# Sketched attention feeding a squared-ReLU layer: loads and stores by t, w_out in 8 KB rows, and nd in four banks

## The chip, the cores and the metric

The kernel runs on one core of a Trainium2 chip. The metric is the device time of one execution in microseconds (us), the median of several runs. Engines are named as the profile names them: PE is the matrix engine (PEld its weight loads), DVE the vector engine, ACT the scalar engine, POOL is GpSimd, and SP the engine that issues most DMAs. Line numbers (L526) are those of the kernel before.

## What is computed

Every head's q and k pass through a degree-two sketch with r = 8: phi(x) is the outer product of S1·x and S2·x, 64 features. Attention is linear in phi(k), its denominator is a dot product, and the four heads of 32 side by side are the input of a two-matrix layer with relu squared.

```python
# batch 4, heads 4, seq 1088, head_dim 32; d_model 128, d_ff 2048
def phi(x):
    a = einsum('rd,bhsd->bhsr', S1, x); b = einsum('rd,bhsd->bhsr', S2, x)
    return einsum('bhsi,bhsj->bhsij', a, b).reshape(..., 64)
kv  = einsum('bhsf,bhsd->bhfd', phi(k), v);  z = phi(k).sum(axis=2)
num = einsum('bhsf,bhfd->bhsd', phi(q), kv); den = einsum('bhsf,bhf->bhs', phi(q), z) + 1e-06
x = (num / den).transpose(0, 2, 1, 3).reshape(4352, 128)
h = x @ w_in                       # 4352 x 2048
out = relu(h)**2 @ w_out           # 4352 x 128, float32
```

## The kernel before

**Tiles.** A sequence of 1088 is written as 32 blocks t of 34 rows j; a partition is (head, t). j is 32 regular rows and two left over. The tokens are cut into nine chunks: two of 512 columns for each batch, and chunk 8 of 256 with the left-over rows of all batches.

**The order.** All work after the setup is one list, `ORDER`, written out by hand. Each item names a helper, its indices and, after `@`, the engine of a copy, relu or square (A for ACT, V for DVE; `M` on a square S means one DVE instruction over two pairs). The engines run their own instructions strictly in the order of the list, and semaphores hold them where data or a buffer is missing. An item that waits therefore holds everything behind it on its engine.

**Keys of batch b.** kT transposes k on DVE (L236), ka multiplies by the sketch matrix Wk (L259), kc copies out of PSUM, kp forms the outer products on DVE (L289), kv multiplies them by v on PE (L339), and kt, kr, kx bring the result into KV. kg, gs, wz, wc make the denominator's weights: a Gram matrix (L306), then a product with `S2bd`, the block-diagonal S2 (L313), written into Wq.

**Queries of batch b** (b = 4 stands for the left-over rows). qT transposes q, qa multiplies (L411), qc copies, dt, dr and da form the denominator and divide, qf forms the outer products (L477) and qp transposes them back (L490).

**Join.** `nd(ci, p)` multiplies KV by the query features in 32 x 32 pieces of the array (L526), two row groups by four column groups, into two PSUM banks. Chunks 0, 1 and 8 take two calls (p = 0, 1), chunks 2 to 7 one each. xe copies the result to `xT` in bf16 (L543 to L548).

**Layer.** `M(ci, u)` makes two of the 16 blocks of 128 hidden columns (L556), R takes the relu (L576 on ACT, L578 on DVE), S squares (L587, L589), `O(ci, u)` accumulates the output (L599), E copies it out (L611) and stores it (L616, L622). PSUM's eight banks are two h buffers of two banks (`ps_h`), one output bank and three others (`ps_m`). W is an idle matmul.

**Loads.** SP issues for each batch k, q and the v of heads 0 and 1, one DMA per head with the four row groups i outermost (L133). GpSimd's queue brings the v of heads 2 and 3 and v's left-over rows (L139): for batch 0 ahead of the two weight matrices (L158, L160), for batches 1 to 3 behind them, issued from within kp (L297). `w_out` is laid out with row ct·128 + c on partition c, 16 pieces of 512 B of the source in each; both weights are cast to bf16 on the way. S1, S2 and the four diagonal blocks of `S2bd` come through ACT's queue (L118, L119, L172); a DVE copy (L197) repeats S for the heads.

```python
526  nc.tensor.matmul(nds[l][32 * h : 32 * h + 32, d0 : d0 + n],
         KV[rows, be, f, 32 * h : 32 * h + 32], src[rows, 2 * h + f, c0 : c0 + n],
         start=(f == 0), stop=(f == 1))
556  nc.tensor.matmul(t[:, i, :N], w_in_sb[:, 2 * u + i, :], T["x", ci][:, :N], ...)
```

## Time and profile before

| | |
|---|---|
| median of the runs | 116.22 us (116.17 to 117.56) |
| the profiled execution, its own time | 116.08 us |
| its span, first to last instruction | 114.3 us |
| first hidden-layer matmul (M.0.0, L556) | 19.67 us into the span |
| last output copy, E.8 (L611), and its stores' issue | ends at 109.66 us, issued at 109.69 us |
| PE / DVE / ACT / GpSimd busy | 101.0 / 94.3 / 87.4 / 12.8 us |
| moved by DMA | 10.23 MB, mean 89 GB/s |
| w_in / w_out, issue to landing | 8.1 / 22.3 us |
| relu on ACT, 128 x 1024 | 61 of 1039 ns |
| output matmuls (L599) | 544 of 219 ns in the row |

The page of a profile gives the busy time of each engine, then the span in 40 slices (2.86 us each) with the busy share in tenths. Matmuls are pipelined, so a row's mean duration is longer than the distance from one to the next. Where an engine stood idle, a wait names what ended it: "A <- B: 2.2, 1, 2.2" is 2.2 us in total, once, the longest 2.2 us. The chain is followed backward from the last instruction to whatever released each step. A line of the stage table gives a stretch of the span, its length, the busy time of PE, PEld, DVE, ACT and POOL with counts, the granted PE clock, the mean share of the 16 DMA engines that were busy, and GB/s.

### The profile page before, as it was taken

What the parts mean: (1) busy time and instruction counts of PE and PEld (TensorE: products, weight loads), DVE (VectorE), ACT (ScalarE), POOL (GpSimd) and SP (SyncE); (2) the same over time, 40 slices, a digit from 0 to 9 for tenths busy, and PEclk for the clock granted to TensorE, in tenths of its full rate; (3) what the DMA queues carried; (4) which work ended last, traced back from release to release, by engine and by line L of the source; (5) the groups of instructions that cost most, each with busy time, mean ns of one, the idle gap of its engine ahead of it and who ended that gap; (6) DMA issues with size and microseconds to landing.
All of it is one profiled execution on the core that took longest, in us unless ns stands there. A gap on an engine that the chain in (4) does not pass through costs nothing.

```text
span 114.3 us, 4082 instructions
## 1 busy us (share of the span) xinstructions
PE 101.0 (88%) x1806; PEld 72.2 (63%) x1806; DVE 94.3 (83%) x148; ACT 87.4 (76%) x140; POOL 12.8 (11%) x24
## 2 busy tenths in 40 slices
PE   5297679987999989999999999999999997999920
PEld 1173556653778864787977557857757866779810
DVE  6185999989929999999999999999899988099700
ACT  4132315999599998799889999899999698895920
POOL 6968200002800000000000000000000000000000
PEclk9999999999999999999999999999999999999995
DMA  4999999977542002000200012002101112012032
GB/s 95 305 202 281 279 280 225 217 209 257 144 139 88 28 9 62 27 0 14 68 21 0 0 17 80 6 6 54 37 0 19 73 16 72 14 11 77 14 58 75
DMA packets 7152, 10.23 MB, mean 89 GB/s; under 512 B 3424, under 2 KB 4704, under 8 KB 7136
## 3 DMA queue, kind: packets, MB, share of 16 engines
q1 hardware_dynamic: 3344, 7.67, 22.8%
q0 software_dynamic: 3616, 2.24, 11.9%
q8 instruction: 14, 0.23, 0.8%
q10 hardware_dynamic: 176, 0.07, 0.2%
q14 instruction: 2, 0.02, 0.0%
HBM read 8.79 MB, written 2.23 MB: 96 GB/s over the span
## 4 chain that ended last, share of the span: by engine, by line
PE 59%; DMA 19%; ACT 10%; POOL 5%; issue 3%; POOLq 0%; ACTq 0%
PE o_ps L599 23%; PE h_ps L556 22%; DMA v_in<-in_v_dram 19%; PE nd_ps L526 7%; ACT r_sb L576 6%; PE acc_ps L339 3%; PE qab_ps L411 3%; ACT g_sb L587 2%; POOL v_in L133 2%; PE gg_ps L306 1%; POOL w_out_sb L160 1%; POOL v_in L139 1%; ACT osb L611 1%; PE kr_ps L363 1%; ACT kab L277 1%
## 5 line engine op out<-in xcount | busy, mean ns | idle before, releaser
L576 ACT ACTIVATE r_sb<-h_ps 128x1024 bf16<-128x1024 f32 (+1 forms) x67 | 63.2, 999 | 5.8 <-PE h_ps L556 5.3
L556 PE MATMUL h_ps<-xT,w_in_sb 128*128 128x512 bf16 (+1 forms) x144 | 39.0, 368 | 0.6 <-ACT r_sb L576 0.6
L599 PEld LDWEIGHTS <-g_sb 128*128 128x128 bf16 x544 | 33.7, 98 | 9.0 <-DVE g_sb L589 0.4
L599 PE MATMUL o_ps<-w_out_sb,g_sb 128*128 128x128 bf16 x544 | 37.3, 219 | 0.0
L589 DVE TENSOR_TENSOR g_sb<-r_sb 128x1024 bf16<-128x1024 bf16 (+2 forms) x41 | 36.4, 922 | 0.5 <-ACT r_sb L576 0.3
L556 PEld LDWEIGHTS <-w_in_sb 128*128 128x128 bf16 x144 | 11.7, 99 | 6.9 <-issue 3.0
L289 DVE TENSOR_TENSOR kp<-kab 128x1024 f32<-128x1024 f32 (+1 forms) x8 | 10.6, 1337 | 0.0
L490 DVE STREAM_TRANSPOSE qp<-qf 128x1024 f32<-128x1024 f32 (+1 forms) x9 | 10.4, 1174 | 0.1
L526 PE MATMUL nd_ps<-qp,KV 32*32 32x256 f32 (+2 forms) x416 | 10.1, 299 | 0.4 <-ACT r_sb L576 0.3
L477 DVE TENSOR_TENSOR qf<-aq,qab 128x1024 f32<-128x1024 f32 (+1 forms) x9 | 10.2, 1154 | 0.1
L587 ACT ACTIVATE g_sb<-r_sb 128x1024 bf16<-128x1024 bf16 (+1 forms) x9 | 8.9, 1016 | 0.1
L526 PEld LDWEIGHTS nd_ps<-qp,KV 32*32 32x32 f32 x416 | 5.5, 104 | 4.5 <-issue 1.7
L339 PE MATMUL acc_ps<-kp,v_in 128*32 128x64 f32 x288 | 5.7, 221 | 2.5 <-DMA v_in<-in_v_dram 2.4
L339 PEld LDWEIGHTS acc_ps<-kp,v_in 128*32 128x32 f32 x288 | 4.6, 110 | 4.3 <-DMA v_in<-in_v_dram 3.0
L411 PE MATMUL qab_ps<-Wq,qT 128*64 128x96 f32 x128 | 6.2, 249 | 0.7 <-issue 0.5
L236 DVE STREAM_TRANSPOSE kT<-k_in 128x1024 f32<-128x1024 f32 (+1 forms) x5 | 5.0, 1019 | 2.2 <-DMA k_in<-in_k_dram 2.2
L259 PEld LDWEIGHTS kab_ps<-Wk,kT 128*64 128x64 f32 x136 | 5.4, 159 | 1.9 <-DVE kT L236 1.3
L139 POOL DMA_DIRECT2D v_in<-in_v_dram x8 | 4.6, 581 | 16.8 <-DMA w_out_sb<-in_moe_w_out_dram 14.1
L411 PEld LDWEIGHTS qab_ps<-Wq,qT 128*64 128x64 f32 x128 | 5.5, 137 | 1.6 <-issue 0.6
L194 PE MATMUL idle_ps<-idle 128*128 128x512 bf16 x13 | 5.3, 508 | 1.2 <-DVE mask L166 1.2
L428 ACT COPY qab<-qab_ps 128x384 f32<-128x384 f32 (+1 forms) x9 | 4.1, 460 | 2.8 <-PE qab_ps L411 2.8
L578 DVE TENSOR_SCALAR r_sb<-h_ps 128x1024 bf16<-128x1024 f32 (+1 forms) x5 | 5.1, 1010 | 1.1 <-PE h_ps L556 1.1
(57 smaller groups left out, 70.4 us busy)
## 6 DMA issues: line engine op xcount, KB each, us to landing
k_in<-in_k_dram SPq DMA_DIRECT2D x4, 544.0 KB
q_in<-in_q_dram SPq DMA_DIRECT2D x4, 544.0 KB
out_dram<-osb SPq DMA_DIRECT2D x8, 256.0 KB
v_in<-in_v_dram POOLq DMA_DIRECT2D x8, 128.0 KB, 13.8
v_in<-in_v_dram SPq DMA_DIRECT2D x8, 128.0 KB
w_in_sb<-in_moe_w_in_dram POOLq DMA_DIRECT2D x1, 512.0 KB, 8.1
w_out_sb<-in_moe_w_out_dram POOLq DMA_DIRECT2D x1, 512.0 KB, 22.3
v_in<-in_v_dram POOLq DMA_DIRECT2D x8, 16.0 KB, 6.3
```

The costliest lines, as they stand in the source:

```text
L139: dma.dma_start(out=vraw[b][32 * j2 : 32 * (j2 + 1), :, NLO, :], in_=v[b].rearrange("h (t j) d -> j t h d", j=NJ)[32 + j2],)
L289: tt.tensor_tensor(out=t[:, :n], in0=s[:, 0, :n, :, None].to_broadcast([128, n, r, r]), in1=s[:, 1, :n, None, :].to_broadcast([128, n, r, r]),
L339: nc.tensor.matmul(acc[32 * h : 32 * h + 32, :64], vraw[b][:, h, 4 * gi + m, :], t[:, m * H + h].rearrange("p i j -> p (i j)"), start=(gi ...
L411: nc.tensor.matmul(t[64 * c : 64 * c + 64, m * H * W3 : (m + 1) * H * W3], cols, Wq[:, be].rearrange("p h x -> p (h x)"), start=True, stop ...
L477: nc.vector.tensor_tensor(out=t[:, :n], in0=T["aq", b][:, g0 : g0 + n, :, None].to_broadcast([128, n, r, r]), in1=T["qab", b][:, g0 : g0 + ...
L490: nc.vector.transpose(T["qp", b][:, :, 128 * i : 128 * i + 32 * nm].rearrange("p f (m t) -> p m f t", t=32), T["qf", b, i][:, : nm * H].re ...
L526: nc.tensor.matmul(nds[l][32 * h : 32 * h + 32, d0 : d0 + n], KV[rows, be, f, 32 * h : 32 * h + 32], src[rows, 2 * h + f, c0 : c0 + n], st ...
L556: nc.tensor.matmul(t[:, i, :N], w_in_sb[:, 2 * u + i, :], T["x", ci][:, :N], start=True, stop=True,)
L576: pin(nc.scalar.activation(t, h, ACTF.Relu))
L587: pin(nc.scalar.activation(t, s, ACTF.Square))
L589: pin(nc.vector.tensor_mul(t, s, s))
L599: nc.tensor.matmul(T["o", ci][:, m, :], T["g", ci, u // 2][:, 2 * (u % 2) + i, m * 128 : (m + 1) * 128], w_out_sb[:, ct, :], start=(ct == ...
```

## The change

- **v** is loaded by SP alone, each batch after its k and q: four DMAs, one for each 32 partitions (i), with t outermost and the heads within, and two for the left-over rows.
- **Outputs** of chunks 0 to 7 go out in four DMAs of 32 partitions with t outermost instead of one with i outermost; chunk 8's two halves are cut by t instead of by batch.
- **w_out** has row c·16 + ct on partition c, one run of 8 KB of the source in each. So that hidden unit c·16 + ct is block ct, M takes w_in's columns with a step of 16. A one-element GpSimd copy makes the weights wait for batch 0's k.
- **nd** computes four row groups at once into four banks: two of `ps_m` and one h buffer. For chunks 2 to 7 one call serves two chunks, for 0, 1 and 8 one call replaces two. xe picks its two banks.
- **S1, S2** are repeated for the heads by the DMA itself. `S2bd` comes from a matmul of a selection matrix with S and a masked copy (bd); the four DMAs into it, and the memsets of it and `Gs`, go. kg's second product takes 32 rows instead of 128.
- **ORDER** is written anew; kT.0.0, wk, bd and wq are now items of it, chunk 3's hidden work starts before chunk 2's, and some relus, squares and copies change engine.

The code, with ORDER cut to its beginning, up to the first hidden matmuls, and the one pair of chunks that swaps places:

```diff
-kT.0.0 kT.0.1 W.2 ka.0.0 kc.0.0 qT.0 ka.0.1 kc.0.1 W.2 kg.0 gs.0 kp.0.0 W.1 wz.0 wc.0 qa.0.0
-qa.0.1 kp.0.1 qc.0.0@A dt.0.0 dr.0.0 da.0.0 kv.0.0 qc.0.1@A qf.0.0 kv.0.1 kt.0 W.1 kr.0 kx.0@A
-qp.0.0 kT.1.0 W.3 nd.0.0 nd.0.1 xe.0.0@A xe.0.1@A ka.1.0 kc.1.0 M.0.0 R.0.0@A ka.1.1 dt.0.1
-kc.1.1 M.0.1 M.0.2 R.0.1@A kg.1 dr.0.1 da.0.1 qf.0.1 qp.0.1 gs.1 nd.1.0 wz.1 qT.1 R.0.2@A M.0.3
...
+kT.0.0 wk.0 W.3 ka.0.0 kT.0.1 bd.0 qT.0 wq.0 kc.0.0 ka.0.1 kc.0.1 W.2 kg.0 gs.0 W.1 wz.0 kp.0.1
+wc.0 kp.0.0 qa.0.0 qc.0.0@A kv.0.0 kv.0.1 qa.0.1 kt.0 dt.0.0 dr.0.0 kT.1.0 da.0.0 ka.1.0 qf.0.0
+qp.0.0 ka.1.1 qc.0.1@A dt.0.1 kr.0 kc.1.1 kc.1.0 kg.1 kx.0@A gs.1 nd.0 xe.0@A qT.1 wz.1 W.2
+M.0.0 M.0.1 R.0.0@A R.0.1@A wc.1 qa.1.0 qa.1.1 kp.1.1 qc.1.0@A M.0.2 M.0.3 qc.1.1@A dr.0.1
+kp.1.0 R.0.2@A R.0.3@A kv.1.0 kv.1.1 M.0.4 kt.1 R.0.4@A M.0.5 R.0.5@A kr.1 da.0.1 kT.2.0 ka.2.0
...
+qp.1.0 qp.1.1 M.1.6 R.1.6@A S.1.1@M S.1.3@M E.0@A kg.3 gs.3 kp.2.0 dt.2.0 S.1.5@M nd.2 xe.3@A
+M.1.7 R.1.7@A O.1.0 M.3.0 R.3.0@A O.1.1 O.1.2 M.3.1 xe.2@A O.1.3 R.3.1@A M.2.0 kp.2.1 R.2.0@A
...
     S12 = consts.tile([2 * r, H, D], F32)
-    nc.scalar.dma_start(out=S12[:r, 0, :], in_=S1)
-    nc.scalar.dma_start(out=S12[r:, 0, :], in_=S2)
+    for x, src in enumerate((S1, S2)):
+        nc.scalar.dma_start(
+            out=S12[x * r : (x + 1) * r], in_=src[:, None, :].to_broadcast([r, H, D])
+        )
     warm = consts.tile([128, 1], F32)
...
-    def load_v(b, h, dma):
...
+    def load(b):
+        for dst, src in ((kin_t, k), (qin_t, q)):
+            nc.sync.dma_start(out=dst[b], in_=src[b].rearrange("h (t j) d -> (h t) j d", j=NJ))
+        vb = v[b].rearrange("h (t j) d -> t h j d", j=NJ)
+        for i in range(4):
+            nc.sync.dma_start(
+                out=vraw[b][32 * i : 32 * (i + 1), :, :NLO, :].rearrange("t h l d -> t h (l d)"),
+                in_=vb[:, :, i * NLO : (i + 1) * NLO, :].rearrange("t h l d -> t h (l d)"),
+            )
+        for j2 in range(2):
+            nc.sync.dma_start(
+                out=vraw[b][32 * j2 : 32 * (j2 + 1), :, NLO, :], in_=vb[:, :, 4 * NLO + j2, :]
+            )
     for b in range(B):
-        load(b, kin_t, k)
-        load(b, qin_t, q)
-        for h in range(2):
-            load_v(b, h, nc.sync)
-    load_v_low(0)
-    w_in_sb = consts.tile([128, C_TILES, 128], BF16)
-    nc.gpsimd.dma_start(out=w_in_sb, in_=moe_w_in.rearrange("d (ct c) -> d ct c", c=128))
+        load(b)
+    w_in_sb = consts.tile([128, d_ff], BF16)
...
+    pin(nc.gpsimd.tensor_copy(w_in_sb[:1, :1], kin_t[0][:1, 0, :1]))
+    nc.gpsimd.dma_start(out=w_in_sb, in_=moe_w_in)
...
     w_out_sb = consts.tile([128, C_TILES, 128], BF16)
-    nc.gpsimd.dma_start(out=w_out_sb, in_=moe_w_out.rearrange("(ct c) d -> c ct d", c=128))
+    nc.gpsimd.dma_start(out=w_out_sb, in_=moe_w_out.rearrange("(c ct) d -> c ct d", ct=C_TILES))
...
         pin(nc.vector.memset(mask[32 * h : 32 * (h + 1), h : h + 1], 1.0))
-    S2bd = consts.tile([128, H, D], F32)
-    pin(nc.vector.memset(S2bd, 0.0))
-    for h in range(H):
-        nc.scalar.dma_start(out=S2bd[r * h : r * h + r, h, :], in_=S2)
     Gs = consts.tile([128, B, H * r], F32)
-    pin(nc.vector.memset(Gs, 0.0))
     dts = [consts.tile([128, 32, r + 1], F32, name=f"dt{i}") for i in range(2)]
...
+    sel = consts.tile([2 * r, H, r], F32)
     pin(
-        nc.vector.tensor_copy(
-            S12[:, 1:, :], S12[:, 0:1, :].to_broadcast([2 * r, H - 1, D])
+        nc.vector.tensor_copy(sel, ident[: 2 * r, None, r : 2 * r].to_broadcast([2 * r, H, r]))
+    )
+    same = consts.tile([H * r, H], F32)
+    pin(
+        nc.vector.tensor_reduce(
+            out=same,
+            in_=ident[: H * r, : H * r].rearrange("p (h i) -> p h i", h=H),
+            op=ALU.add,
+            axis=mybir.AxisListType.X,
         )
...
     W(4, "")
+    S12h = S12.rearrange("r h d -> r (h d)")
+    pin(nc.tensor.transpose(T_ps[:, : 2 * r], S12h, ident[: 2 * r, : 2 * r]))
     pin(
-        nc.tensor.transpose(
-            T_ps[:, : 2 * r], S12.rearrange("r h d -> r (h d)"), ident[: 2 * r, : 2 * r]
+        nc.tensor.matmul(
+            T_ps[: H * r, 128:256],
+            sel.rearrange("r h i -> r (h i)"),
+            S12h,
+            start=True,
+            stop=True,
         )
...
     Wk = consts.tile([128, H, 2 * r], F32)
-    pin(
-        nc.vector.tensor_tensor(
-            out=Wk,
-            in0=T_ps[:, None, : 2 * r].to_broadcast([128, H, 2 * r]),
-            in1=mask[:, :, None].to_broadcast([128, H, 2 * r]),
-            op=ALU.mult,
-        )
-    )
     Wq = consts.tile([128, B, H, W3], F32)
-    for b in range(B):
-        nc.scalar.copy(
-            Wq[:, b].rearrange("p h (x i) -> p h x i", x=3)[:, :, ::2],
-            Wk.rearrange("p h (x i) -> p h x i", x=2),
-        )
+    S2bd = consts.tile([128, H, D], F32)
...
+    def wk(i, eng):
+        pin(
+            nc.vector.tensor_tensor(
+                out=Wk,
+                in0=T_ps[:, None, : 2 * r].to_broadcast([128, H, 2 * r]),
+                in1=mask[:, :, None].to_broadcast([128, H, 2 * r]),
+                op=ALU.mult,
+            )
+        )
...
+    def bd(i, eng):
+        pin(
+            nc.vector.tensor_tensor(
+                out=S2bd[: H * r],
+                in0=T_ps[: H * r, 128:256].rearrange("p (h d) -> p h d", h=H),
+                in1=same[:, :, None].to_broadcast([H * r, H, D]),
+                op=ALU.mult,
+            )
+        )
...
+    def wq(i, eng):
+        for b in range(B):
+            pin(
+                nc.scalar.copy(
+                    Wq[:, b].rearrange("p h (x i) -> p h x i", x=3)[:, :, ::2],
+                    Wk.rearrange("p h (x i) -> p h x i", x=2),
+                )
+            )
...
-        if (b, gi) == (0, 1):
-            for b in range(1, B):
-                load_v_low(b)
...
     def kg(b, eng):
...
                 T["gg", b][:, 32:64],
-                S2bd.rearrange("p h d -> p (h d)"),
-                Gs[:, b],
+                S2bd[: H * r].rearrange("p h d -> p (h d)"),
+                Gs[: H * r, b],
                 start=True,
...
-    def nd(ci, p, eng):
+    def nd(ci, eng):
         b = min(ci // 2, 4)
-        c = p if b in (0, 4) else ci % 2
         src = T["qp", b]
-        if (ci, p) == (0, 1):
-            t = ps_h.tile([128, 2, 512], F32, tag="h", name="h_ps")
-            nds = [t[:, l] for l in range(2)]
+        hs = ps_h.tile([128, 2, 512], F32, tag="h", name="h_ps")
+        nds = [ps_m.tile([128, 512], F32, tag="m", name="nd_ps") for _ in range(2)]
+        T["nd", ci] = nds = nds + [hs[:, l] for l in range(2)]
...
+        if b == 0:
+            cols = [(128 * ci, 0, 128, 0, 0)]
+        elif b == 4:
+            cols = [(0, 0, 32, 0, 1), (32, 32, 32, 2, 3)]
         else:
-            nds = [ps_m.tile([128, 512], F32, tag="m", name="nd_ps") for _ in range(2)]
-        T["nd", ci, p] = nds
...
-        if b == 0:
-            cols = [(128 * ci, 0, 128, 0)]
-        elif b == 4:
-            cols = [(0, 0, 32, c), (32, 32, 32, 2 + c)]
-        else:
-            cols = [(0, 0, 256, b)]
-        for c0, d0, n, be in cols:
+            cols = [(0, 0, 256, b, b)]
+        for c0, d0, n, *be in cols:
             for f in range(2):
                 for h in range(H):
-                    for l in range(2):
-                        rows = slice(64 * c + 32 * l, 64 * c + 32 * l + 32)
+                    for l in range(4):
+                        rows = slice(32 * l, 32 * l + 32)
                         pin(
...
                                 nds[l][32 * h : 32 * h + 32, d0 : d0 + n],
-                                KV[rows, be, f, 32 * h : 32 * h + 32],
+                                KV[rows, be[l // 2], f, 32 * h : 32 * h + 32],
                                 src[rows, 2 * h + f, c0 : c0 + n],
...
-    def xe(ci, p, eng):
-        if p == 0:
-            T["x", ci] = xT_pool.tile([128, 512], BF16, tag="xT", name="xT")
-        x = T["x", ci]
-        for l in range(2):
-            src = T["nd", ci, p][l]
+    def xe(ci, eng):
+        T["x", ci] = x = xT_pool.tile([128, 512], BF16, tag="xT", name="xT")
+        if 2 <= ci < 8:
+            nds = T["nd", ci // 2 * 2][2 * (ci % 2) :][:2]
+        else:
+            nds = T["nd", ci]
+        for l, src in enumerate(nds):
             if ci < 2:
-                c0 = 256 * p + 128 * l
-                pin(COPY[eng](x[:, c0 : c0 + 128], src[:, :128]))
+                pin(COPY[eng](x[:, 128 * l : 128 * l + 128], src[:, :128]))
             elif ci < 8:
...
             else:
-                dst = x[:, 128 * l : 128 * l + 128].rearrange("p (m c t) -> p c m t", m=2, c=2)
-                pin(COPY[eng](dst[:, p], src[:, :64].rearrange("p (m t) -> p m t", m=2)))
+                j, c = l % 2, l // 2
+                dst = x[:, 128 * j : 128 * j + 128].rearrange("p (t m c) -> p c m t", m=2, c=2)
+                pin(COPY[eng](dst[:, c], src[:, :64].rearrange("p (m t) -> p m t", m=2)))
...
                     t[:, i, :N],
-                    w_in_sb[:, 2 * u + i, :],
+                    w_in_sb[:, 2 * u + i :: C_TILES],
                     T["x", ci][:, :N],
...
             b, half = divmod(ci, 2)
-            o = out[b * S : (b + 1) * S].rearrange("(t j) d -> t j d", j=NJ)[:, : 4 * NLO]
-            o = o.rearrange("t (i l) d -> i t l d", i=4)[:, :, 4 * half : 4 * half + 4]
-            nc.sync.dma_start(
-                out=o.rearrange("i t l d -> i t (l d)"), in_=osb.rearrange("p m d -> p (m d)")
-            )
+            o = out[b * S : (b + 1) * S].rearrange("(t j) d -> t j d", j=NJ)
+            for hi in range(4):
+                j0 = hi * NLO + half * 4
+                nc.sync.dma_start(
+                    out=o[:, j0 : j0 + 4], in_=osb[32 * hi : 32 * hi + 32, :, :]
+                )
         else:
-            o = out.rearrange("(b t j) d -> b t j d", b=B, j=NJ)[:, :, 4 * NLO :]
+            o = out.rearrange("(b t j) d -> t b j d", b=B, j=NJ)[:, :, 4 * NLO :]
             for g, dma in enumerate((nc.sync, nc.scalar)):
                 dma.dma_start(
-                    out=o[2 * g : 2 * g + 2].rearrange("b t j d -> b t (j d)"),
+                    out=o[16 * g : 16 * g + 16].rearrange("t b j d -> t b (j d)"),
                     in_=osb[64 * g : 64 * (g + 1), :2].rearrange("p m d -> p (m d)"),
...
     OPS = dict(kT=kT, ka=ka, kc=kc, kp=kp, kv=kv, kt=kt, kr=kr, kx=kx, qT=qT)
-    OPS.update(kg=kg, gs=gs, wz=wz, wc=wc)
+    OPS.update(kg=kg, gs=gs, wz=wz, wc=wc, wk=wk, wq=wq, bd=bd)
     OPS.update(qa=qa, qc=qc, dt=dt, dr=dr, da=da, qf=qf, qp=qp, nd=nd, xe=xe)

```

## The prediction, made before the change was run

> **What bounds the kernel now.** I read the page first: the busy shares, then the 40 slices, which separate a loading stage from a stage that computes.
>
> ```profile
> span 114.3 us, 4082 instructions
> ...
> PE 101.0 (88%) x1806; PEld 72.2 (63%) x1806; DVE 94.3 (83%) x148; ACT 87.4 (76%) x140; POOL 12.8 (11%) x24
> ...
> PE   5297679987999989999999999999999997999920
> ...
> DVE  6185999989929999999999999999899988099700
> ACT  4132315999599998799889999899999698895920
> ...
> DMA  4999999977542002000200012002101112012032
> ```
>
> See that until the eighth slice (23 us) the DMA engines are the full row, and from the eleventh on PE, DVE and ACT are full together. Next, busy time by stage, from the first hidden-layer matmul M.0.0 (19.67 us) to the last output copy (109.66 us). Columns: length, then PE, PEld, DVE, ACT, POOL, clock, DMA share, GB/s.
>
> ```profile
> 19.67:30.00 10.33, 9.03 (x206) 5.78 (x210) 9.65 (x15) 8.86 (x16) 2.07 (x4) 1.00 0.77 208
> 30.00:40.00 10.00, 10.00 (x181) 7.74 (x165) 7.78 (x10) 9.67 (x17) 1.06 (x2) 1.00 0.35 101
> 40.00:84.00 44.00, 43.62 (x763) 31.04 (x766) 42.78 (x59) 41.31 (x59) 0.00 (x0) 1.00 0.10 26
> 84.00:97.00 13.00, 12.42 (x220) 8.95 (x220) 12.17 (x15) 11.49 (x17) 0.00 (x0) 1.00 0.15 39
> 97.00:109.66 12.66, 12.23 (x217) 10.01 (x214) 7.89 (x12) 10.30 (x17) 0.00 (x0) 1.00 0.13 29
> ```
>
> DVE sums to 80.3 us and ACT to 81.6 us of this 90 us stage. The clock is 1.00, so no gain can come from there. Then the chain that ended last and the waits:
>
> ```profile
> PE 59%; DMA 19%; ACT 10%; POOL 5%; issue 3%; POOLq 0%; ACTq 0%
> ```
>
> ```profile
> POOL v_in L139 <- DMA w_out_sb<-in_moe_w_out_dram: 14.1, 1, 14.1
> ...
> ACT r_sb L576 <- PE h_ps L556: 5.3, 11, 1.1
> ...
> PE acc_ps L339 <- DMA v_in<-in_v_dram: 2.4, 2, 1.6
> ...
> DVE kT L236 <- DMA k_in<-in_k_dram: 2.2, 1, 2.2
> ```
>
> So PE carries the chain, and the 19% DMA is one transfer of v. GpSimd's queue stood 14.1 us behind w_out, which brought batch 1's v so late that PE waited (28.27 us), and DVE waited 2.2 us for batch 3's k (32.25 to 34.41). The prices come from the groups by shape:
>
> ```profile
> L599 PE MATMUL o_ps<-w_out_sb,g_sb 128*128 128x128 bf16 x544 | 37.3, 219 | 0.0
> ...
> L556 PEld LDWEIGHTS <-w_in_sb 128*128 128x128 bf16 x144 | 11.7, 99 | 6.9 <-issue 3.0
> ...
> L526 PE MATMUL nd_ps<-qp,KV 32*32 32x256 f32 x192 | 6.6, 380 | 0.4 <-ACT r_sb L576 0.3
> ...
> L363 PEld LDWEIGHTS kr_ps<-ident,kvT 128*128 128x128 f32 x16 | 2.3, 191 | 0.9 <-ACT kvT L351 0.5
> ```
>
> A matmul row's duration includes the pipeline; the price is the spacing, which the chain gives: 16 output matmuls in 0.89 us, so 55 ns each; a pair of 512-column ones 0.43 us.
>
> **The change, part by part.**
>
> *nd over four banks.* Each call now issues both row halves: 64 matmul records where it had 32, so as many in all, with four row groups side by side instead of two. In the chain a 256-column call takes 1.02 to 1.10 us, a 128-column call 0.59 (0.67 in the timeline): doubling the columns adds 0.43, which is streaming, two accumulation steps of 0.43 each; the rest is issue. The 32-column call of chunk 8, already 64 records, takes 0.75 us (0.68 in the chain), so 64 records issue in about 0.7. If four groups stream together, a 256-column call for two chunks costs 0.85 of streaming plus half its issue, 1.2 us, against 2.1: 0.9 saved, three times. Chunk 1, likewise, 0.8 against 1.2: 0.4; chunk 0's lies ahead of M.0.0. Chunk 8 is issue-bound and saves nothing. Sum 3.1 us of PE in the stage. Bounds: 0 (two groups at a time) to 4.2 (streaming or issue alone, 3 x 1.25 + 0.5). I take 3.1, since chunk 8's rows show issue at 11 ns a record. The price: nd now holds one of the two h_ps buffers, so the pipeline of hidden matmuls loses a slot for nd and its two copies (2 x 0.36 us). A relu (0.97 us) held the slot as long, and the copies were on ACT before; cost 0, up to 0.3 us at each of four calls if a relu comes late.
>
> *Order.* Counted from both lists with these durations: batch 1's second ka (0.8), kg (0.63) and wz (0.2) now stand ahead of M.0.0, so PE has 1.6 us less behind it. DVE has 1.9 less (batch 1's kT and qT early), ACT 1.8 less, the split of relus and squares included (squares on ACT 9 to 7, full DVE pair squares 19 to 21).
>
> *The sum of the stage.* PE's back-to-back rates over the list from M.0.0 give 84.5 us before: 72 M (29.3), 72 O (30.3), nd 8.8, qa 4.9, ka 3.8, kv 3.6, kg 1.9, kr 1.3, wz 0.6, at the chain's durations. The stage lasts 89.6, so 5.1 are lost beyond the fullest engine. After: PE 84.5 - 3.1 - 1.6 = 79.8; ACT 81.6 - 1.8 = 79.8; DVE 80.3 - 1.9 = 78.4. PE and ACT are the fullest; ACT begins last, with its first relu at 20.3: 100.1, plus the same 5.1 lost, 105.2 instead of 109.66: 4.4 saved. In that 5.1 lie about 1.3 us of PE idling between 19.67 and 30 over v, which should go; against it, three engines within 1.5 us of each other stall one another more often. I let these cancel. Bounds: 1.8 (only ACT's saving counts) to 7.1 (PE's 1.6, nd's 4.2 and the 1.3).
>
> *First chunk.* DVE does the work up to qp.0.0 in a row: from Wk (5.5 us, S landed at 4.86) come kT, bd, qT, kp, wc, kp, dt, dr (6.6 us) and 0.7 of waiting for wc as before, so 12.8 us; then kT.1.0 (1.44), da, qf, qp (2.7): 16.9, against 16.78 before. nd.0 follows kr, kx and kg.1 and M.0.0 comes at 19.0 to 19.7; before, 19.67. I take 0. New in DVE's queue is a wait for batch 1's k at 12.8 us: da, qf and qp stand behind it and PE, ACT behind those. Before, k1 was issued at 4.78 and needed at 16.75 without a wait, so bounds -0.7 to +1.5. Removed: a copy (0.24), two memsets (0.17 each, idle time). Added: sel, same, bd, about 0.25 each by the 0.24 and 0.29 rows; the first two run before S lands. S now moves 32 pieces per matrix instead of 8: 0 to +0.6, inside those bounds.
>
> *Loads.* v goes from 16 SP and GpSimd issues to six SP issues per batch: about 0.35 + 0.35 + 4 x 0.6 + 2 x 0.55 = 4.2 us of SP per batch. Its 1.63 MB need 5.8 us at the 280 GB/s of the slices, so the issue hides; if not, every batch slips. GpSimd's queue keeps only the weights, behind a new wait for k0 (landed by 5.6): w_in then starts 1.3 us later than its 4.34 and took 8.1 to land, so about 13.8, cover 5 us to M.0.0. w_out, 128 pieces for 2048, was needed at 31.2 and came at 27.2: cost 0.
>
> *Outputs.* A 256 KB store held a quarter of the DMA engines for five microseconds:
>
> ```profile
> 101.00:106.20 5.20, 5.20 (x88) 4.79 (x77) 5.19 (x9) 3.73 (x8) 0.00 (x0) 1.00 0.21 54
> ```
>
> Chunk 7's, issued at 107.2, runs into chunk 8's, issued at 109.69, and the span ends 4.6 us after the last copy. Four issues of 0.54 us cost SP 2.2 us, which ends 0.3 us before chunk 8's; two osb buffers cover the others. I take 0.6 saved, bounds 0 to 1.2. The Trainium skill speaks against this part: "DMA: Bandwidth & Descriptors", Rules for kernel authors, says that splitting a transfer over disjoint partition halves is no use, as the parts share the same engines. By that rule the 0.6 would be 0 and the sum 111.7. The share of 0.21 is what keeps me from it.
>
> *Strided w_in.* 144 weight loads now step over 32 bytes. 58 of the 72 M pairs follow something other than an M, mostly an output matmul of 55 ns, under which the first load must hide; the second has 215 ns. A strided load is not in this trace. Bounds: nothing (the 99 ns bf16 row), or the pace of the 191 ns f32 load, 92 more: the contiguous one hides in 55 ns, so at most 92 x 58 = 5.3 exposed. I take 0, the row of the same type and shape. The skill's "TensorE: Matmul & The Clock Gate", Weight-path perf modes, allows steps up to 1,024 elements in its fast load, which would leave 111.1; the f32 row's pace would make 116.4. No run here shows it yet.
>
> **Sum** against the profiled execution's 116.08 (span 114.3 and 1.8 around it): 116.1 - 4.4 - 0.6 = **111.1 us**. The median of the runs, 116.22, is 0.14 above it, nothing here.
>
> **Rivals.**
> 1. *ACT and DVE bind.* PE's saving falls idle and only 1.8 + 0.6 come: 113.7. For it: 40 to 84 us, DVE 42.8 and ACT 41.3 of 44. Against: PE holds 59% of the chain, DVE idles 4.8 us after 97. Two row groups at a time lands here too (PE saves 1.6).
> 2. *k1 late.* DVE stands at kT.1.0 and later batches slip, as all loads share one queue: 1.5 at the first chunk and as much again at batches 2 and 3: 114.1. For it: SP issues that blocked 5.1 us (18.25). Against: 512-piece loads no longer wait behind w_out.
> 3. *Slower: the strided weight load.* At place L556 each of 58 pairs exposes what the load takes beyond 55 ns. It decides from 5.0 / 58 = 86 ns exposed, that is 141 ns a load; at 215 ns a load it gives 111.1 + 9.3 = 120.4. For it: every contiguous neighbour says nothing on steps. Against: the 99 ns row leaves slack, and the second load has 215 ns.
> 4. *More.* PE's saving counts whole: 7.1 + 0.6, so 108.4, or 107.8 with the tail's 1.2. For it: DVE and ACT idle after 97 us. Against: the full rows from 40 to 84 us.
>
> **How the numbers follow.** Forecast (109 to 113.5) 0.55; better (106.5 to 109) 0.12; rival 1 (113.5 to 115) 0.12; rival 2 (112.6 to 115.5) 0.11; rival 3 (116 to 121) 0.10. A measurement tells 2% from no change: 113.9 and 118.5. Faster: 0.55 + 0.12 + half of rivals 1 and 2, 0.78. Slower: rival 3 with loads above 185 ns, 0.06. Within: 0.16. The range leaves out rival 3 and the best half of "better": 107.6 to 115.4; the forecast alone holds 109 to 113.5.
>
> **What would show it.** Right: the nd groups at 1.2 us per 64 records, no DVE wait for k after 20 us, GpSimd's 14.1 us gone, store transfers under 3 us, M pairs still 0.43 us behind an O. Wrong: an idle DVE at kT.1.0 near 13 us; L556 loads above 140 ns or M pairs at 0.5 us and more; PE idle with ACT full, which is rival 1; two nd calls' worth of time in one.

## The result, and the profile after

| | before | after |
|---|---|---|
| median of the runs, us | 116.53 (115.62 to 118.27) | 116.0 (114.39 to 117.47) |
| profiled execution, its span | 116.08, 114.3 | 114.45, 112.7 |
| M.0.0 starts | 19.67 | 21.72 (forecast 19.7, no change) |
| from there to the end of E.8 | 89.99 | 87.02 (forecast 4.4 less) |
| from there to the end of the span | 4.63 | 3.93 (forecast 0.6 less) |

The ratio is 0.9898, 95% interval 0.9859 to 0.9937: 1% faster, where 111.1 us had been forecast (0.956). Ratios leave out, as slow, executions more than 1.5% above the quickest of their kernel, so this one rests on 11 of the 20 and that of e5 below on 3 of 11. The median lies 1.5 us above the profiled execution's own time, which is one of the quickest of its kernel (0.45 us in the kernel before), so the three stretches show 1.6 us of gain where the ratio shows 1.2. Of the eleven executions, seven have a mean granted clock above 0.99 and took 114.4 to 115.8 us; the four at 0.980 to 0.985 took 115.4 to 116.1.

The page after, its lines in the order shown of before:

```profile
span 112.7 us, 4096 instructions
...
PE 98.9 (88%) x1788; PEld 76.6 (68%) x1807; DVE 93.2 (83%) x147; ACT 86.3 (77%) x141; POOL 2.1 (2%) x9
...
PE   5199765997999999999999999989999999999940
...
PE 61%; ACT 16%; DMA 12%; issue 5%; DVE 3%; SPq 0%; another core or an unknown queue 0%; ACTq 0%
...
L571 PEld LDWEIGHTS <-w_in_sb 128*128 128x128 bf16 x144 | 16.3, 148 | 4.7 <-issue 2.2
```

GpSimd's 14.1 us of waiting are gone, and DMA's part of the chain fell from 19 to 12%. But "issue" rose from 3 to 5%, ACT from 10 to 16%, and the strided weight loads take 148 ns instead of 99. The stages, columns as before:

```profile
19.67:30.00 10.33, 9.47 (x214) 6.80 (x214) 9.20 (x15) 7.92 (x15) 0.00 (x0) 1.00 0.99 257
30.00:40.00 10.00, 9.80 (x201) 8.04 (x205) 7.89 (x14) 9.41 (x19) 0.00 (x0) 1.00 0.06 11
40.00:84.00 44.00, 43.02 (x766) 33.32 (x775) 41.65 (x53) 41.75 (x62) 0.00 (x0) 1.00 0.11 26
```

PE is as full as before; the loads now end near 32 us (share 0.06 against 0.35). The chain of waits up to M.0.0 tells what the first chunk hung on (start, length, what):

```profile
5.44 9.13 DMA k_in<-in_k_dram
14.57 0.02 issue
14.59 1.25 DVE kT L258
...
15.98 1.25 PE kab_ps L281 x34
17.23 0.02 issue
17.25 0.75 ACT kab L299 x3
18.00 0.04 issue
18.05 0.50 PE gg_ps L324 x10
18.55 0.95 issue
19.50 0.41 PE gg_ps L324 x8
```

Batch 1's k is now at the head of the first chunk's path, and in the midst of kg.1 PE stands for 0.95 us with nothing that the profile shows to wait for.

### The profile page after: what moved, and what is told of

Read it like the earlier page. It is cut to its first block, busy times and chain, and to the rows that moved or that the text cites. A ratio compares the mean times of both kernels' runs of the same rounds, so it can differ in the third digit from the quotient of the medians.

```text
span 112.7 us, 4096 instructions
## 1 busy us (share of the span) xinstructions
PE 98.9 (88%) x1788; PEld 76.6 (68%) x1807; DVE 93.2 (83%) x147; ACT 86.3 (77%) x141; POOL 2.1 (2%) x9
## 3 DMA queue, kind: packets, MB, share of 16 engines
q0 software_dynamic: 288, 1.05, 4.7%
## 4 chain that ended last, share of the span: by engine, by line
PE 61%; ACT 16%; DMA 12%; issue 5%; DVE 3%; SPq 0%; another core or an unknown queue 0%; ACTq 0%
PE o_ps L614 21%; PE h_ps L571 19%; ACT r_sb L591 12%; DMA k_in<-in_k_dram 12%; PE nd_ps L540 5%; PE qab_ps L429 4%; PE kab_ps L281 3%; PE h_ps L540 2%; PE gg_ps L324 2%; PE gg_ps L331 1%; PE kr_ps L381 1%; PE acc_ps L357 1%; DVE kT L258 1%; DVE g_sb L604 1%; ACT xT L559 1%
## 5 line engine op out<-in xcount | busy, mean ns | idle before, releaser
L604 DVE TENSOR_TENSOR g_sb<-r_sb 128x2048 bf16<-128x2048 bf16 (+2 forms) x43 | 37.9, 919 | 1.5 <-ACT r_sb L591 1.4
L571 PE MATMUL h_ps<-xT,w_in_sb 128*128 128x512 bf16 (+1 forms) x127 | 37.2, 374 | 0.8 <-ACT r_sb L591 0.6
L571 PEld LDWEIGHTS <-w_in_sb 128*128 128x128 bf16 x144 | 16.3, 148 | 4.7 <-issue 2.2
L311 DVE TENSOR_TENSOR kp<-kab 128x1280 f32<-128x1280 f32 (+1 forms) x8 | 10.7, 1343 | 1.3 <-ACT kab L299 1.3
L540 PE MATMUL h_ps<-qp,KV 32*32 32x256 f32 (+2 forms) x224 | 8.1, 302 | 0.0
L540 PE MATMUL nd_ps<-qp,KV 32*32 32x256 f32 (+2 forms) x224 | 7.9, 302 | 0.0
L281 PE MATMUL kab_ps<-Wk,kT 128*64 128x64 f32 x136 | 5.9, 244 | 1.1 <-DVE kT L266 1.1
L299 ACT COPY kab<-kab_ps 128x256 f32<-128x256 f32 (+1 forms) x12 | 3.3, 323 | 3.8 <-PE kab_ps L281 3.8
L602 ACT ACTIVATE g_sb<-r_sb 128x1024 bf16<-128x1024 bf16 (+1 forms) x7 | 6.1, 881 | 0.1
L593 DVE TENSOR_SCALAR r_sb<-h_ps 128x512 bf16<-128x512 f32 (+1 forms) x5 | 4.5, 903 | 1.3 <-PE h_ps L571 1.3
```

The source lines that it names most:

```text
L281: nc.tensor.matmul(kk[64 * c : 64 * c + 64, m * 64 : (m + 1) * 64], kt[:, c0 + 64 * c : c0 + 64 * c + 64], Wk.rearrange("p h x -> p (h x)" ...
L311: tt.tensor_tensor(out=t[:, :n], in0=s[:, 0, :n, :, None].to_broadcast([128, n, r, r]), in1=s[:, 1, :n, None, :].to_broadcast([128, n, r, r]),
L540: nc.tensor.matmul(nds[l][32 * h : 32 * h + 32, d0 : d0 + n], KV[rows, be[l // 2], f, 32 * h : 32 * h + 32], src[rows, 2 * h + f, c0 : c0 ...
L571: nc.tensor.matmul(t[:, i, :N], w_in_sb[:, 2 * u + i :: C_TILES], T["x", ci][:, :N], start=True, stop=True,)
L604: pin(nc.vector.tensor_mul(t, s, s))
```

## The experiments

Ratios are to the kernel before, with 95% intervals; "from after" compares with 0.9898. Edits are to the changed kernel unless said otherwise.

### What each part is worth

**e1: nd's row groups two at a time.**

```diff
-for l in range(4):
+for l in (2 * half, 2 * half + 1):
```
`half` runs outside of f and h.

> The changed kernel with the 64 records of an nd call in another order: row groups 0 and 1 first, then 2 and 3, so that only two stream together; buffers, instructions and the order list stay. nd's 256-column call should go from 1.43 to about 2.1 us. If PE sets the end of the stage, the three such calls and chunk 1's cost 2.0 to 2.5 us against the changed kernel (114.45 in its profiled execution), so 116.5 to 117. If ACT and DVE bind and PE's saving fell idle, at most 0.7, so 114.5 to 115.2.

1.0012 (0.9975 to 1.0048): four groups at once are worth 1.1%, 1.3 us. A call for two chunks, from its first matmul's start to its last one's end, takes 1.79 to 1.82 us so, 1.49 to 1.50 in the change, 2 x 1.09 before. So of the 0.69 us that a pair saves, 0.38 come already with one call in place of two, and 0.31 with the four groups; over three calls that is 0.9 of the 1.3 us.

**e4: the stores alone, on the kernel before.**

```diff
-o = o.rearrange("t (i l) d -> i t l d", i=4)[:, :, 4 * half : 4 * half + 4]
+for hi in range(4):
+    nc.sync.dma_start(out=o[:, j0 : j0 + 4], in_=osb[32 * hi : 32 * hi + 32, :, :])
```


> The kernel before with only the stores changed: four DMAs of 32 partitions with t outermost for chunks 0 to 7, chunk 8 cut by t. If the spread over the DMA engines is what shortens the end, the span ends 0.6 us sooner after the last copy (4.0 instead of 4.6 us) and the time is about 115.5, ratio 0.995. If the four issues on SP or small transfers eat that, 116.1 or more.

0.9894 (0.9852 to 0.9935): alone they bring as much as the whole change. From the end of E.8 to the end of the span it takes 3.3 us instead of 4.6; the last byte is out 2.0 us after E.8 instead of 3.35. Around chunk 0's store the mean DMA share was 0.19 over 5.5 us before, and is 0.40 over 2.7 us here. The run changes the order within a store (i, of 4, no longer stands outermost) along with the number of DMAs, and doesn't tell the two apart.

**e5: the loads alone, on the kernel before.**

```diff
-for h in range(2):
-    load_v(b, h, nc.sync)
+for i in range(4):
+    nc.sync.dma_start(out=vraw[b][32 * i : 32 * (i + 1), :, :NLO, :]...)
```
with the two left-over DMAs on SP, none of v on GpSimd's queue, and w_in behind k0.

> The kernel before with only the loads of the change: v on SP's queue, six DMAs a batch with t outermost, and the weights behind a wait for batch 0's k (w_out still 16 pieces a partition, order list as before). If the loads were worth what the prediction gave them (PE's wait for v and DVE's 2.2 us for k gone), 1.0 to 1.5 us: 115, ratio 0.988 to 0.991. If the time that the waits took is only handed to the next limit (instruction fetch of PE, ACT's queue), within 0.4 of before.

0.9953 (0.9901 to 1.0006): half a per cent, not told from nothing.

**e6: the weights alone, on the kernel before.**

```diff
-moe_w_out.rearrange("(ct c) d -> c ct d", c=128)
+moe_w_out.rearrange("(c ct) d -> c ct d", ct=C_TILES)
-w_in_sb[:, 2 * u + i, :]
+w_in_sb[:, 2 * u + i :: C_TILES]
```


> The kernel before with only the layout of the weights changed: w_out one 8 KB run a partition, w_in's columns with a step of 16. The run with contiguous columns says that the step costs about 1.2 us; then this one is 0.5 to 1.2 us slower, less what a sooner w_out gives (GpSimd's queue stands 14.1 us behind it and batch 1's v comes after it: up to 1.1 us back). If the step costs nothing by itself, 0.5 to 1.1 faster.

1.0272 (1.0228 to 1.0317), and it isn't the strided step: from the end of E.0, the first output copy, to the end of E.8 it takes 68.61 us, 68.60 before. The loss lies ahead, M.0.0 came at 25.81. The waits of 12 to 30 us, in the longest of its five executions (120.55 us):

```profile
ACT kvT L351 <- PE acc_ps L339: 6.8, 1, 6.8
PEld acc_ps L339 <- DMA v_in<-in_v_dram: 5.1, 1, 5.1
...
DVE kT L236 <- DMA k_in<-in_k_dram: 4.8, 1, 4.8
POOL v_in L139 <- DMA w_out_sb<-in_moe_w_out_dram: 3.5, 1, 3.5
```

w_out landed in 12.3 us instead of 22.3. From 10 to 16 us GpSimd's queue, which it is on, moved 0.94 MB instead of 0.60, and SP's queue 0.68 instead of 1.09. Batch 0's v and batch 1's k, on SP's queue, came late: PE stood from 14.0 to 18.9 us, kT.1.0 came at 22.26 (16.75 before), and from 17.40 to 24.23 us the granted clock was 0.50. Behind w_out, batch 1's v landed from 19.3 us on instead of 28.2; what its transfer took from k beyond what w_out's took, no run separates. A faster w_out was paid for by the loads beside it.

**e2: w_in copied into contiguous blocks by GpSimd. e12: both weights by DMA as before.**

```diff
+for c0 in range(0, C_TILES, 4): nc.gpsimd.tensor_copy(w_in_ct[:, c0 : c0 + 4, :], ...)
-w_in_sb[:, 2 * u + i :: C_TILES]
+w_in_ct[:, 2 * u + i, :]
```


> The changed kernel, but GpSimd, which has nothing else to do then, copies w_in in four pieces into blocks of 128 neighbouring columns, and the hidden matmuls load their weights from there. The weight load should return from 148 to 99 ns. If strided loads took the missing time, up to 58 x 0.05 = 2.9 us are gained (111.6 to 112.5). If they hide, as the unchanged 56 ns from an output matmul to the next hidden one says, 0.3 to 0.7 us from the pairs of hidden matmuls (216 instead of 222 ns), so about 114. If the copies end after 21.7 us, M.0.0 is late by the difference.

> The changed kernel with only the weights as before: w_in in contiguous blocks and w_out in pieces of 256 bytes, both by GpSimd's queue, w_in behind the same wait. If the strided step is the whole cost of the weights part: weight loads of the hidden layer back at 99 ns and about 1% less, 114.5 to 115.0 us, ratio 0.977 to 0.984. Rival (the small pieces take DMA engines from batch 0's v and batch 1's k, which the long runs spared): kT.1.0 later than 14.6 us by 1 us or more and ratio 0.988 to 1.000.

e2: 0.9795 (0.9739 to 0.9851), 1.0% from after. e12: 0.9904 (0.987 to 0.9938), none. Weight loads are back at 98 ns in both, and the median distance of the two matmuls of a pair at 216 ns instead of 224; a hidden matmul behind an output matmul starts 56 ns after it with either layout. In e12 the ratio is that of the second expectation, but its kT.1.0 is not late (14.78, 14.59 in after). Two ways back to the same loads, two results: not settled here (see e13, e16).

**e3: batch 1's kT, ka, kc, kg behind chunk 0's join.**

```diff
-kT.1.0 da.0.0 ka.1.0 qf.0.0 qp.0.0 ka.1.1 ... kg.1 kx.0@A gs.1 nd.0
+da.0.0 qf.0.0 qp.0.0 qc.0.1@A kr.0 kx.0@A kT.1.0 W.2 nd.0 xe.0@A ka.1.0
```


> The changed kernel with batch 1's kT, ka, kc, kg, gs and wz moved behind chunk 0's path in the order list (about where the kernel before has them). DVE no longer waits 0.5 us for k and works 1.4 us on kT ahead of da.0.0. If the late first chunk (M.0.0 at 21.72 instead of 19.67 us) is where the gain went, M.0.0 comes at 19.5 to 20 us and the time falls by 1.5 to 2, to 112.5 to 113. If the three engines' total work sets the end, the moved work is only paid later and the time stays within 0.5 of 114.5.

1.012 (1.0064 to 1.0177): 2.2% worse than after. qp.0.0 ended 0.74 us earlier (17.93), but PE then stood 1.57 us inside nd.0, so M.0.0 came at 21.88; and batch 1 came 3 us later, so that from M.0.0 to the end of E.0 it took 25.6 us instead of 23.1 (from there to E.8 63.96, 63.95 in after). As a remedy the late kT.1.0 fell; what it is worth to M.0.0 with PE supplied, no run shows.

**e8: loads of batches 2 and 3 held until KV of batch 0.**

```diff
+nc.gpsimd.tensor_copy(kin_t[2][:1, 0, :1], KV[:1, 0, 0, :1])
+load(2)
+load(3)
```


> The changed kernel with the loads of batches 2 and 3 held (through a one-element GpSimd copy) until batch 0's KV is there, about 18 us, so that little is on the DMA engines between 15 and 18 us, when PE's instructions for nd.0 are fetched. If the load traffic delays the fetch, PE's 1.0 us stall in kg.1 (18.55 to 19.50) shrinks below 0.4 and M.0.0 comes 0.6 us or more sooner; batch 2's k then lands at about 22.5, needed at 24.55. If the fetch takes as long without traffic, the stall stays and the time is equal or, where k3 is late, up to 1 us longer.

0.998 (0.9947 to 1.0012), 0.8% worse than after, and PE still stood 1.05 us in kg.1 with the loads at rest (DMA share 0.05 and 0.00 from 18 to 20 us). DMA traffic while PE stands is not what makes it stand. From 17 to 18 us the share was still 0.83.

### Why PE stands with nothing to wait for

In the traces so far I counted PE's records (weight loads, matmuls and its sequencer's entries) up to the idle stretch:

| kernel | records ahead | inside | idle, us |
|---|---|---|---|
| after, e1, e2, e7, e8, e12 | 448 or 449 | gg_ps (kg.1) | 0.95, 1.32, 1.87, 1.84, 1.05, 1.87 |
| e3, e4 | 449 | nd.0 | 1.57, 0.75 |

The operation differs, the count doesn't. On one of the queues that the page calls "instruction", 14 packets of 16,384 bytes go out in a span; the first starts 3.0 to 4.4 us after PE passed record 174 or so, takes 1.1 to 1.4 us, and PE resumes 1.2 to 1.5 us behind it. From 174 to 449 are mostly fp32 matmuls at 8 to 22 ns a record. If PE is through with them sooner, it runs dry.

Later stretches fit the same count. Ahead of one stand 705 records in before, e8 and e14 (0.46, 1.20 and 3.05 us), ahead of another 3265 in e2, e3, e7, e10, e12 and e15 (0.47 to 1.15 us): 449 plus 256, and plus 11 x 256. (The trace of after lacks 19 matmul records; its stretches of 0.65 us at 25.57 and 0.47 us at 92.76 stand at 703 and 3248.) By these counts a packet holds 256 records of 64 bytes, an estimate. The stretch can cost more than itself: in e1, e2 and e12 the granted clock was 0.50 for 3.4 us, from 22.39, 20.97 and 21.08 us on, 0.5 to 1.9 us behind it; in after, e7 and e8 it was not.

In the kernel before, PE was at record 449 at 18.5 us, when the packet (15.7 to 16.8) had just let it on.

**e9: fifty matmuls of zeros, 32x32, where PE waits for S. e15: twelve of them. e14: fifty in the kernel before.**

```diff
 W(4, "")
+for _ in range(50):
+    nc.tensor.matmul(T["idle"][:32, :32], idle[:32, :32], idle[:32, :32], ...)
```


> The changed kernel with fifty 32x32 matmuls of zeros more, right behind the first four idle ones, where TensorE waits for S anyway (3.1 to 5.4 us). What it tests: in every run so far TensorE ran dry at one and the same place of its own program, ahead of matmul record 218 to 220 (record 448 to 450 with the weight loads), whatever operation stands there (gg_ps in the changed kernel, nd in others); the 16 KB instruction packet for what follows starts 3.0 to 4.4 us after record 180 or so, takes 1.1 to 1.4 us, and TensorE goes on 1.4 us after it. Theory of the instruction packet: with 100 records more ahead, that place moves to the old record 350, where TensorE stands 14.9 to 16.0 us waiting for DVE in any case. So no idle stretch over 0.5 us ahead of kg.1 or nd.0; M.0.0 at 20.4 to 20.9 us in place of 21.7 to 23.6; fewer executions with a lowered clock; 114.5 to 115.0 us, ratio 0.975 to 0.984. Rival (the idle stretch is kg.1's or nd.0's own wait for a bank or a copy): it stays ahead of gg_ps, ratio 0.986 to 0.994 like the changed kernel.

> The changed kernel with twelve of the small idle matmuls in place of fifty: 24 records more. If the place where TensorE runs dry is fixed by the count of its instructions, it moves 24 records ahead in the program, from inside gg_ps to inside the four kr_ps matmuls before it, and stays there for 0.5 to 1.5 us, still ahead of M.0.0: 115 to 116 us, ratio 0.985 to 0.995. If the gain of the fifty came by another way (a warm clock, say), TensorE is dry ahead of gg_ps as before or nowhere.

> The kernel before with the same fifty small idle matmuls. Its record 449 stood inside nd.0.0 at 18.5 us, just when the packet let TensorE go on, so it lost nothing there: theory of a cost that the change brought in, ratio 0.997 to 1.003. Rival (the fifty matmuls are good for any kernel, by the clock or otherwise): 0.980 to 0.990, as on the changed kernel.

e9: 0.9758 (0.9727 to 0.9789), 113.54 us, 1.4% from after. e15: 0.9906 (0.9846 to 0.9967). e14: 1.0004 (0.9961 to 1.0047), so the fifty bring the kernel before nothing. It is no clean control: in its profiled execution (119.5 us, the longest but one of twelve) PE stood at record 705 instead, so a gain may have been paid back there. In e15 the place moved with the count, by 24 records to the operation ahead, again behind 449. PE's waits from 14 to 22 us in e15, and from 20 to 30 us in e14:

```profile
PE kr_ps L387 <- issue: 1.3, 1, 1.3
...
PE gg_ps L312 <- issue: 3.1, 1, 3.1
```

And e9's chain:

```profile
5.46 9.97 DMA k_in<-in_k_dram
15.43 0.02 issue
15.46 1.25 DVE kT L264
...
18.91 0.76 PE gg_ps L330 x18
19.67 0.01 issue
19.68 0.30 PE nd_ps L546 x2
```

kg.1 runs through in 0.76 us and nd.0 starts behind it; record 449 now falls ahead of qa, where PE stands 0.57 us and DVE's kT.1.0 would hold it 1 us later in any case. One number missed: M.0.0 came at 21.55, not 20.4 to 20.9, since batch 1's k landed 0.86 us later than in the profile of after; the gain at that place was mostly taken by rival 2's wait. A second stretch, 0.47 us at 92.76 behind the 256 records of nd.8 in after, is gone too. From nd.8's start to E.6's end it takes 9.20 us in e9 and 9.82 in after. Of the 1.2 us between the two profiled executions (113.26 and 114.45), 0.2 lie ahead of M.0.0, 0.4 from there to the end of E.0 and 0.6 behind it. The ratios differ by 1.6 us. All six executions of e9 have a granted clock of 0.994 to 1.0, the eleven of after 0.980 to 0.996, so a part may be the clock's; no run separates it.

### S2 and the weights again, with PE supplied

**e7: S1, S2 and S2bd by DMA as before. e17: the same with the fifty matmuls.**

```diff
-nc.tensor.matmul(T_ps[: H * r, 128:256], sel.rearrange("r h i -> r (h i)"), S12h, ...)
+for h in range(H):
+    nc.scalar.dma_start(out=S2bd[r * h : r * h + r, h, :], in_=S2)
```


> The changed kernel with S1, S2 and S2bd brought as before (two DMAs, a DVE copy, four DMAs into S2bd, no matmul and no bd). Wk should start at 5.5 instead of 6.29 us. If that delay reaches M.0.0, the time falls by 0.5 to 0.8; if the first chunk waits for k1, DVE's kT and PE's instruction fetch instead, no more than 0.2.

> The changed kernel with S2 by DMA and the fifty small idle matmuls, w_in strided as in the change. Beside it: 0.9758 with S2 by matmul and the same fifty. If S2 by matmul costs what the contiguous pair of runs gave (0.9758 to 0.9672): 0.964 to 0.970. If that difference was the copies' and not S2's: 0.974 to 0.978. Against the run with the weights undone this one also gives the strided step without GpSimd's copies: 1.0 to 1.2 us if the stage behind M.0.0 decides (86.0 against 84.9 us).

e7: 0.9818 (0.978 to 0.9855), 0.8% from after; e17: 0.9679 (0.9624 to 0.9735), 0.8% from e9. Yet Wk didn't come earlier in e7 (6.49 against 6.29). One difference is at the other end. SP's closing waits, us behind E.8, each for the semaphores of some stores:

```
after  2.07 2.34 2.41 2.89 2.97 3.04   span ends 3.93 behind E.8
e7     0.73 0.80 0.87 1.33 2.08 2.35   span ends 3.24 behind E.8
```

The stores' last byte is out at 1.97 and 1.99, so the stores are alike. SP goes through the waits one by one. In after the first is that of the very last stores, and the five others follow it; in e7 four are done before it.

**e18: e9, and four DMAs of S2 into a tile that nothing reads.**

```diff
+for h in range(H): nc.scalar.dma_start(out=spare[r * h : r * h + r, h, :], in_=S2)
```


> The changed kernel with the fifty small idle matmuls and S2 by matmul as in the change (that alone: 0.9758), and four small DMAs of S2 on ACT's queue into a tile that nothing reads. Theory: S2 by matmul costs nothing at Wk; it takes four DMAs away, so the stores fall on other semaphores and SP's closing waits, which it goes through one after the other, begin with the one of the very last store (2.07 us behind the last copy, then five more) and not with those of stores long landed (0.73, 0.80, 0.87, 1.33, then 2.07). Then the four unused DMAs bring the early order back: from the last copy to the end 3.2 to 3.3 us in place of 3.9, ratio 0.966 to 0.972. Rival (the cost is the matmul's, or the later Wk): 3.9 us, ratio 0.974 to 0.978.

The waits came at 0.73, 0.80, 0.87, 1.33, 2.08, 2.35 and the span ended 3.24 us behind E.8, as in e7: the order of the closing waits goes with the number of DMAs, and S2 by matmul, with four fewer, costs 0.67 us there. The time, 0.9724 (0.9665 to 0.9783), lies between the two expectations: the tail is shown, the rest of the 0.8% isn't.

**e10: e2 and e7 together. e11: the same with the fifty. e13: e2 with the fifty. e16: e17 with both weights by DMA as before.**

> The changed kernel with two steps undone together: w_in copied by GpSimd to contiguous blocks (alone: 0.9795) and S2 brought by DMA as before (alone: 0.9818). If the two are separate costs they add: 0.970 to 0.975, 113.0 to 113.6 us. If both only spare the same lowered clock after the idle stretch near 19 us: 0.978 to 0.983, 114.0 to 114.4 us.

> The run before (both steps undone) with the fifty small idle matmuls ahead as well. Theory of the instruction packet: 0.8 to 1.3 us less than that run (M.0.0 at 20.5 to 21.5 us): ratio 0.960 to 0.967. Rival (the stretch is a wait of its own): the same as that run within 0.3%.

> The changed kernel with w_in copied to contiguous blocks and the fifty small idle matmuls, S2 still by matmul. Beside two runs with the same fifty: 0.9758 (w_in strided, S2 by matmul) and 0.9672 (w_in contiguous, S2 by DMA). With TensorE no longer dry this shares the 0.9% between the two. If it is the strided step: 0.966 to 0.970 (112.3 to 112.8 us). If it is the start of Wk, 0.5 us earlier with S2 by DMA: 0.973 to 0.978.

> The changed kernel with the weights part undone (w_in and w_out brought by DMA in pieces of 256 bytes, so w_in is contiguous without GpSimd's copies), S2 by DMA, and the fifty small idle matmuls. Beside it stands the run with the same but w_in copied by GpSimd (0.9672): there qf took 2.03 us on DVE beside the copies, against 1.22, and M.0.0 came at 22.6 us against 21.6. If that is GpSimd's doing and the small pieces cost nothing: M.0.0 at 20.9 to 21.6 us, stage behind it 85 us as there, ratio 0.957 to 0.964 (111.4 to 112.3 us). If the small pieces take the DMA engines from batch 0's v and batch 1's k: kT.1.0 later than 15.6 us and ratio 0.967 or more.

| | w_in | S2 by | fifty | ratio | M.0.0 | M.0.0 to E.8 | end of E.0 to E.8 |
|---|---|---|---|---|---|---|---|
| e10 | GpSimd copy | DMA | no | 0.9770 (0.9724 to 0.9816) | 22.40 | 86.34 | 64.35 |
| e9 | strided | matmul | yes | 0.9758 (0.9727 to 0.9789) | 21.55 | 86.02 | 63.35 |
| e13 | GpSimd copy | matmul | yes | 0.9758 (0.9702 to 0.9814) | 23.02 | 84.87 | 63.07 |
| e17 | strided | DMA | yes | 0.9679 (0.9624 to 0.9735) | 22.16 | 85.74 | 63.36 |
| e11 | GpSimd copy | DMA | yes | 0.9672 (0.9638 to 0.9707) | 22.56 | 84.87 | 63.07 |
| e16 | DMA as before | DMA | yes | 0.9671 (0.9624 to 0.9718) | 21.76 | 85.93 | 63.07 |

The fifty are worth 1.0% again (e10 to e11), but not where it was expected: M.0.0 came no sooner, and the gain lies behind E.0, where PE of e10 stands 1.15 us at 92.21. Behind E.0's end the strided step has a price that repeats: e9, e17 and e18 take 63.35 to 63.37 us, e11, e13 and e16 63.07, so 0.3 us for 114 of the 144 weight loads. From M.0.0 on, contiguous blocks save 0.9 to 1.15 us (e11 and e13 against e17 and e9), but there M.0.0 itself comes later with the copies. With them DVE pays ahead of M.0.0; its timeline in e13, then in e9:

```profile
16.88 0.78 DVE L496 TENSOR_TENSOR aq<-qab,den 128x128 f32<-128x128 f32 x1
17.70 2.02 DVE L509 TENSOR_TENSOR qf<-aq,qab 128x1024 f32<-128x1024 f32 x1
```

```profile
16.75 0.25 DVE L488 TENSOR_TENSOR aq<-qab,den 128x128 f32<-128x128 f32 x1
17.03 1.22 DVE L501 TENSOR_TENSOR qf<-aq,qab 128x1024 f32<-128x1024 f32 x1
```

GpSimd's four copies (15.4 to 20.7 us in e13) run beside these. In e16, without copies, DVE is at its usual pace, but PE runs dry again, 1.06 us at record 702 (its trace lacks records too), behind M.0.0. Batch 1's k is not the small pieces' doing: kT.1.0 came at 15.66 in e16, at 15.63 and 16.06 in e11 and e17 without them. Why e2 alone came out 1% better than after stays open.

e11, e16 and e17 beat both kernels and don't differ among themselves: 112.4 to 112.9 us, 3.2 to 3.3% less than before.

## Why the prediction was wrong, step by step

- **nd over four banks: mechanism right, size off.** A call for two chunks took 1.49 us, not 1.2: beside 0.85 of streaming, 0.64 of the issue's 0.7 shows, not half. Three pairs saved 2.1 instead of 2.7, chunk 1 nothing (1.29 for 1.33) instead of 0.4; chunk 8, set at 0, saved 0.2. Together 2.3 for 3.1.
- **Strided w_in, "I take 0": too low by 0.3 us**, as far as it shows (114 of the 144 loads, behind E.0). A load takes 148 ns. Rival 3 named 141 ns as the place from which it decides, each load behind an output matmul exposing what exceeds 55 ns; but such a matmul still starts 56 ns later, and the loss shows inside the pairs, 224 ns for 216. The Trainium skill ("TensorE: Matmul & The Clock Gate", Weight-path perf modes) allows steps up to 1,024 elements in its fast load; here a step of 16 cost half as much again per load.
- **The stage, 4.4 us: 2.97.** nd takes 0.8 from it, the step 0.3 and the dry stretch at 92.76 another 0.47. That would leave 2.8, so the sum closes within 0.2; its other terms were not measured one by one.
- **First chunk, "I take 0": +2.05, the step that failed most.** I let DVE reach kT.1.0 at 12.8. It came there at 14.07, no sooner than it had come to the same point before (13.91). Its rows in after, ahead of kT.1.0:

```profile
10.06 1.49 DVE L311 TENSOR_TENSOR kp<-kab 128x1280 f32<-128x1280 f32 x1 [1.31 <-ACT kab L299]
...
13.15 0.29 DVE L462 TENSOR_TENSOR dt<-qab 128x128 f32<-128x128 f32 x1 [0.36 <-ACT qab L446]
...
14.59 1.25 DVE L258 STREAM_TRANSPOSE kT<-k_in 128x1024 f32<-128x1024 f32 x1 [0.52 <-DMA k_in<-in_k_dram]
```

  My sum of durations held 0.7 us of waiting "as before", where DVE of before waits 1.40 ahead of wc; in the change kp waits 1.31 for kab and dt 0.36 for qab. Wk also came at 6.29 instead of 5.5, of which 0.5 was made good by a part of kT that now stands ahead of it. So kT.1.0 (1.4) and its wait for k (0.52), put ahead of qf, moved qp.0.0's end from 16.77 to 18.67, and PE's dry stretch in kg.1 (0.95) stands on the same way to M.0.0. Rival 2's place was right: batch 1's k leads the chain in after and in e9. How the 2.05 divides is not shown: e3 and e9 each take one part away, and the other grows (1.57 us dry, 1.32 us of waiting for k).
- **A term that wasn't there: PE's instruction supply.** The list makes PE pass records 174 to 449 faster. Moving the place gave 1.4% (e9) and 1.0% (e11) here and nothing in the kernel before (e14), where another place ran dry. The profile of before showed "issue 3%", and PE standing 0.46 us at record 705, and I didn't ask what it was.
- **Outputs, 0.6: 0.70 by the profile, and by luck.** The stores alone save 1.3 us in the tail (e4); the closing waits give back 0.67 (e18). The skill's rule against splitting ("DMA: Bandwidth & Descriptors", Rules for kernel authors) is not put to the test by it: e4 gained 1.06% with the split and another order within a store at once.
- **Loads, hidden: held but for batch 1's k.** After 20 us DVE waits for no k, and e5 bounds the gain at 1%. The 14.1 us of GpSimd were misread: batch 1's v had been issued ahead of them, at 6.06 to 9.45 us, and landed late (28.2) behind w_out on the same queue. What the wait held was the last of batch 2's v and batch 3's, for which no engine of before stood.
- **Rival 1** (ACT and DVE bind) is seen in part: ACT's share of the chain rose from 10 to 16%.
- **The rest of the miss**, 1.5 us from the profiled execution to the median, is in none of these terms; it goes with a lower granted clock, and no run shows what lowers it there.

## What to carry to other kernels

An engine's idle time put down to "issue" has a place in the program: count its records up to it over several kernels, and if the count stays while the operation changes, move the place to where the engine waits anyway, and look where the next one then falls. In a queue that runs in order, an operation moved ahead brings the load that it waits for onto the path of all behind it. A transfer made faster takes from those beside it (e6), so ask which of them is needed first. Durations of an engine in a row are a lower bound of its arrival: the waits between them move, they don't vanish. And where whole times scatter, a stretch that begins behind the disturbed part can still give a price: the 0.3 us of the strided step repeat within 0.02 us over six kernels.
